# Attention and low-rank mixer in one kernel: the opening reordered, low-rank rows taken out of PSUM by ScalarE, V converted a step sooner, and narrower score tiles from step nine

## The chip, the cores and the metric

The kernel runs on one core of a Trainium2 chip. The metric is the device time of one execution in microseconds, as the median of several runs. TensorE does the matrix products, VectorE (DVE), ScalarE (ACT) and GpSimd (POOL) the element-wise work, and SyncE (SP) issues most of the DMAs; a few are issued by ScalarE.

## The reference, cut to what matters

A causal linear attention with a decay per head runs over blocks of 64 rows, and its output, with the heads side by side, goes through a low-rank mixing over the sequence and a two-layer product with a relu:

```
q, k, v: 4 batches x 8 heads x 768 rows x 64;  lam: one decay per head, 0.97 to 0.99
for each block of 64 rows:
    intra = ((q k^T) * D) v          D[i, j] = lam^(i - j) where i >= j, else 0
    inter = (q * lam^(i + 1)) state
    state = lam^64 * state + (k * lam^(63 - i))^T v
x = the heads side by side: 4 x 768 x 512
h = x^T U V                          U: 768 x 32, V: 32 x 768
u = x + h^T
out = u + relu(u w1) w2              w1: 512 x 2048, w2: 2048 x 512
```

U, V, w1 and w2 arrive as 64-bit floats, whose two 32-bit words the kernel loads and turns into 32-bit floats itself.

## The kernel before, in words

**Attention.** The kernel works on blocks of 128 rows, six for each of the four batches: 24 steps, s = 0 to 23. The order of the instructions is written out by hand: the list `pieces` (L546 to L567) names for each step what is issued, and each engine works through its own queue in that order. In a step the pieces are:

- `prep(s + 1)`: TensorE transposes the next block of q and k into one PSUM bank each (tags pq and pk, L348), ScalarE copies them out (L351). For step 0 this is done in two halves, ahead of the list, by `turn_half` (L663 and L668).
- `scale(s + 1)`: GpSimd multiplies q's transpose by powers of lam, `qs` (L376), and the k of the step after by others, `ks` (L365). The powers come from VectorE: `constants` makes the decay mask by eight scans (L302), `rev` is its last column (L671), and `powers` makes `powq` by four more scans (L314).
- `mix`, `low`, `low_rows`, `next_of_low`: the low-rank part, see below.
- `intra(s)`: TensorE multiplies the masked scores by v (L446), ScalarE copies the sum out (L451).
- `state(s)`: TensorE makes the state's increment into `pkv` (L411), which shares the bank pk; VectorE adds the faded old state (L419, or copies in L417).
- `scores(s + 1)` (L393), `inter(s + 1)` (L434, reading `qs` and the state), `masked(s + 1)` (VectorE, L402) and `fade(s + 1)` (ScalarE, L385).
- `aside(s)`: pieces of the conversion of U, V and two tiles of w1, by a table of steps (L624 to L628). What they give to ScalarE is put off to `late`, in the next step. A conversion of 64-bit words is L154, L155 (VectorE), L160, L161 (ScalarE), L171, L179, L184 (VectorE); V's split follows in L598 (VectorE), two casts in L605 on ScalarE and two on VectorE, and subtractions in L609 on VectorE and GpSimd.
- `turn(s - 7)`: transposes a finished block of u (L516) and splits it (L521, L532, L535, L536).

**Low-rank part.** After each batch, in steps 6, 12 and 18 and a fourth time among the first units of the next stage, `low` sums x^T U into the bank pq (or a bank b2, the fourth time), as four groups of 32 rows and 128 columns (L461). `low_rows` takes the high bits out of PSUM into the temporary `p_h`, four VectorE instructions of 32 x 128 (L474). `next_of_low` then issues, at three places, two ScalarE copies (L485, L486), four VectorE subtractions that read PSUM again (L480), and one ScalarE copy (L489). `mix` (L499) reads all of these as one operand `p_hl`.

**Temporaries.** `tmp` hands out three buffers in turn (L99) to `p_h`, to `ut` in `turn` and, in the later blocks, to `uf` too. In those later blocks (from block 16) GpSimd's L529 reads `ut` and `uf`.

**Products.** With the attention nearly done, `hidden` runs u w1 in three passes of 32-bit products split into parts (L718, L728; ScalarE and VectorE take the sums out in L724 and L733), with the rest of the low-rank part between its products (L773 to L784). Then the second product (L851, L853, L855) ends the kernel.

**Opening.** The core asks for q by SyncE and for k by ScalarE, then for lam by ScalarE (L652 to L654). Matmuls on a block of zeros keep TensorE occupied (`keep_busy`, L661, L666). lam is spread over all partitions by a product with ones (L665) and copied by VectorE (L669).

Of the kernel before, what the change touches and what calls it, by code (L numbers as in the profile page):

```python
# [10 lines left out]
U32 = mybir.dt.uint32  # L11
AF = mybir.ActivationFunctionType
ALU = mybir.AluOpType
# [5 lines left out]
def kernel(  # L19
# [68 lines left out]
    def set_ends(t):  # L88
        nc.vector.memset(t[:, 0:1], 1151.0)
        nc.vector.memset(t[:, 1:2], 255.0 * (1 << 23))  # L90
        ends.append(t)
# [6 lines left out]
    def tmp(name):  # L98
        return wconv.tile([P, C], FP32, tag="tmp", bufs=3, name=name)  # L99
# [145 lines left out]
    def two_banks(name, tag):  # L245
        return psf.tile([P, 2, N], FP32, tag=tag, name=name)
# [14 lines left out]
    def parts(s):  # L261
        return 2 if s == 0 else 1
# [44 lines left out]
    def powers():  # L307
        nc.vector.memset(zeros, 0.0)
        for x in range(2):
            nc.vector.tensor_copy(  # L310
                out=lamh[x * D : (x + 1) * D, :], in_=lamb[x * D : (x + 1) * D, x::2]
            )
        for a in range(HP):
            nc.vector.tensor_tensor_scan(  # L314
                powq[:, a, :], lamh[:, a : a + 1].broadcast_to([P, P]),
                zeros.broadcast_to([P, P]), 1.0, ALU.mult, ALU.add,
            )
# [13 lines left out]

    def keep_busy(n):

        out = two_banks("idle", "px")[:, 0, 0:P]
        for i in range(n):
            nc.tensor.matmul(out=out, lhsT=blank, rhs=blank, start=True, stop=True)

    qts, kts = {}, {}

# [11 lines left out]
        nc.scalar.copy(ts[s][:, a0 : a0 + n, :], pt)  # L351

    def prep(s):
        for a0 in range(0, HP, HP // parts(s)) if s > 0 else ():
            for name in "qk":
                turn_half(s, a0, name)
        st[s].update(qt=qts.pop(s), kt=kts.pop(s))
        for name in "qk":
            load_next(name)
# [27 lines left out]
    def scores(s):  # L387
        qt, kt = st[s]["qt"], st[s]["kt"]
        st[s]["pss"] = pss = two_banks("pss", "pss").rearrange("p x (a i) -> p x a i", a=HP)
        for a in range(HP):  # L390
            for x in range(2):
                for rows in half if s >= 2 * NT else [slice(0, P)]:
                    nc.tensor.matmul(  # L393
                        out=pss[rows, x, a, :], lhsT=kt[half[x], a, rows],
                        rhs=qt[half[x], a, :], start=True, stop=True,
                    )
# [70 lines left out]

    def low_rows(b):

        pp, t = pps.pop(b), tmp("p_h")[0:R]  # L470
        h, h2, l, l2 = (p_hl[g * R : (g + 1) * R] for g in range(G))
        own = [(slice(g * R, (g + 1) * R), slice(g * P, (g + 1) * P)) for g in range(G)]
        for rows, cols in own:
            nc.vector.tensor_scalar(  # L474
                t[:, cols].bitcast(U32), pp[rows].bitcast(U32), HI, None, ALU.bitwise_and
            )

        def low_part():
            for rows, cols in own:
                nc.vector.tensor_tensor(  # L480
                    out=l[:, cols], in0=pp[rows], in1=t[:, cols], op=ALU.subtract
                )

        def spread():
            nc.scalar.copy(h, t)  # L485
            nc.scalar.copy(h2, t)  # L486

        def spread_low():
            nc.scalar.copy(l2, l.bitcast(FP32))  # L489

        pps[b] = [spread, low_part, spread_low]
# [52 lines left out]


    pieces = [("prep", 0), ("scale", 0), ("scores", 0), ("inter", 0), ("masked", 0)]  # L546
    pieces += [("powers", 0)]
    for s in range(NS):
        b, c = divmod(s, NT)
        done = s - NT - 1  # L550
# [19 lines left out]
    def load_next(name, engine=nc.sync):  # L570
        if waiting[name]:
            load(name, waiting[name].pop(0), engine)
# [3 lines left out]
        "prep": prep, "fade": fade, "scores": scores, "masked": masked, "inter": inter,  # L576
        "intra": intra, "state": state,
        "low": low, "low_rows": low_rows, "next_of_low": next_of_low, "mix": mix, "turn": turn,
        "scale": scale, "powers": lambda s: powers(), "turned": lambda s: turned.pop(s)(),
    }  # L580
    def v_steps():

        st = {}

        def dst():
            if "v" not in st:
                st["v"] = wconv.tile([P, C], FP32, tag="wf", name="vf")[0 : 2 * R, 0:SH]
            return st["v"]

        def parts(gs):  # L590
            for half in range(2):
                rows, cols = slice(half * R, (half + 1) * R), slice(half * SH, (half + 1) * SH)
                for g in gs:
                    yield v_hl[g * R : (g + 1) * R, cols], rows

        def five():
            st["t"] = t = wconv.tile([P, C], FP32, tag="wt", name="vt")[0 : 2 * R, 0:SH]
            nc.vector.tensor_scalar(  # L598
                t.bitcast(U32), st["v"].bitcast(U32), HI, None, ALU.bitwise_and
            )  # L600
            on_scalar(lambda: high(0))

        def high(g, copy=nc.scalar.copy):
            for out, rows in parts((g,)):
                copy(out, st["t"][rows])  # L605

        def low(g, engine):
            for out, rows in parts((g,)):
                engine.tensor_tensor(  # L609
                    out=out, in0=st["v"][rows], in1=st["t"][rows], op=ALU.subtract  # L610
                )

        halves = [moe_V[:, half * SH : (half + 1) * SH] for half in range(2)]
        return weight_steps(dst, halves, SH, 2 * R, in_parts=True) + [
            five, lambda: low(1, nc.vector), lambda: high(2, nc.vector.tensor_copy),
            lambda: low(3, nc.gpsimd),
        ]
# [5 lines left out]
    side = {}  # L623
    for steps, at in (  # L624
        (u_side, (-1, 1, 1, 2, 2)),
        (v_steps(), (0, 0, 3, 3, 4, 4, 4, 5, 4, 5)),
        (w1_steps(0, True), (3, 4, 5, 6, 8, 9, 10, 11, 12, 13, 14)),
        (w1_steps(1, True), (8, 9, 10, 11, 15, 16, 17, 18, 19, 20, 21)),  # L628
    ):
        assert len(steps) == len(at)  # L630
        for step, n in zip(steps, at):
            side.setdefault(n, []).append(step)
# [16 lines left out]
    nc.vector.memset(blank, 0.0)  # L649
    nc.vector.memset(lam_row[:, H:], 1.0)  # L650
    set_ends(vp[:, S + C : S + C + 2].bitcast(FP32))
    load_next("q", nc.sync)  # L652
    load_next("k", nc.scalar)
    nc.scalar.dma_start(out=lam_row[:, 0:H], in_=lam.unsqueeze(0))  # L654
    for name in "qkvkv":
        load_next(name)
    aside(-1)
    for name in "qkv":
        load_next(name)
    make_identity(nc, ident)  # L660
    keep_busy(4)  # L661
    for name in "qk":
        turn_half(0, 0, name)  # L663
    pl = two_banks("pl", "pss")[:, 0, 0:H]
    nc.tensor.matmul(out=pl, lhsT=lam_row[:, H:], rhs=lam_row[:, 0:H], start=True, stop=True)  # L665
    keep_busy(1)  # L666
    for name in "qk":
        turn_half(0, HP // 2, name)  # L668
    nc.vector.tensor_copy(out=lamb, in_=pl)  # L669
    constants()  # L670
    nc.vector.tensor_copy(out=rev, in_=mask[:, :, :, P - 1])  # L671
    scale_k(0)
    run.update(aside=aside, late=on_scalar_late)
# [280 lines left out]
```

## Time and profile before

| what | us |
|---|---|
| median of six runs | 676.73 |
| lowest and highest run | 676.59, 677.12 |
| the profiled execution | 677.31 |
| its span, first to last instruction | 675.5 |
| TensorE, matmuls, busy | 666.0 |
| VectorE busy | 499.0 |
| ScalarE busy | 277.3 |
| GpSimd busy | 113.8 |

All views are of one profiled execution, and times in them count from the start of its span. In a timeline row the columns are start, duration, engine and line, the operation, the written and the read tile, the shape and the count of instructions merged in the row; in brackets stands how long the engine was idle before and what ended the wait. PEld is the loading of weights, which runs beside matmuls. A matmul of 32-bit floats shows as two instructions. In the table by stretches the columns are the stretch, its length, then the busy time of TensorE, its weight loads, VectorE, ScalarE and GpSimd with instruction counts, TensorE's granted clock, the DMA share and GB/s.

### The profile page before, as it was taken

What the parts mean: (1) busy time and instruction counts of PE and PEld (TensorE: products, weight loads), DVE (VectorE), ACT (ScalarE), POOL (GpSimd) and SP (SyncE); (2) the same over time, 40 slices, a digit from 0 to 9 for tenths busy, and PEclk for the clock granted to TensorE, in tenths of its full rate; (3) what the DMA queues carried; (4) which work ended last, traced back from release to release, by engine and by line L of the source; (5) the groups of instructions that cost most, each with busy time, mean ns of one, the idle gap of its engine ahead of it and who ended that gap; (6) DMA issues with size and microseconds to landing.
All of it is one profiled execution on the core that took longest, in us unless ns stands there. A gap on an engine that the chain in (4) does not pass through costs nothing.

```text
span 675.5 us, 13172 instructions
## 1 busy us (share of the span) xinstructions
PE 666.0 (99%) x5124; PEld 545.1 (81%) x5124; DVE 499.0 (74%) x879; ACT 277.3 (41%) x513; POOL 113.8 (17%) x92
## 2 busy tenths in 40 slices
PE   8999999999999999999999999999999999999997
PEld 7888898787888888888888888888888888888886
DVE  4689999777999777777798255786586776865864
ACT  4665767544555444444455132232232322322320
POOL 3446767331000000000000000030030200300300
PEclk9999999999999999999999999999999999999999
DMA  9998994164777655565577999854353363453431
GB/s 213 209 232 222 230 224 128 49 221 142 252 264 243 234 202 203 202 203 203 202 251 258 317 320 376 308 176 159 94 203 108 110 201 95 150 162 95 158 91 62
DMA packets 131775, 131.27 MB, mean 194 GB/s; under 512 B 81346, under 2 KB 89794, under 8 KB 131714
## 3 DMA queue, kind: packets, MB, share of 16 engines
q1 hardware_dynamic: 130656, 130.18, 60.9%
q8 instruction: 40, 0.66, 0.4%
q10 hardware_dynamic: 1058, 0.26, 0.2%
q14 instruction: 21, 0.17, 0.1%
HBM read 80.09 MB, written 50.33 MB: 193 GB/s over the span
## 4 chain that ended last, share of the span: by engine, by line
PE 94%; DVE 3%; ACT 1%; issue 0%; DMA 0%; DVEq 0%; ACTq 0%
PE pz L718 27%; PE pz L853 13%; PE pz L851 13%; PE pd L728 13%; PE pd L855 13%; PE px L446 3%; PE pss L393 3%; PE put L516 2%; PE pq L348 1%; PE px L434 1%; PE pkv L411 1%; PE pk L348 1%; DVE sm L402 1%; PE pp L461 1%; PE pu L499 1%
## 5 line engine op out<-in xcount | busy, mean ns | idle before, releaser
L718 PE MATMUL pz<-u_hl,w 128*128 128x512 f32 x768 | 190.3, 397 | 0.7 <-ACT x_nat L451 0.7
L718 PEld LDWEIGHTS pz<-u_hl,w 128*128 128x128 f32 x768 | 144.0, 188 | 36.0 <-ACT x_nat L451 0.8
L853 PE MATMUL pz<-w_hl,m 128*128 128x512 f32 x384 | 151.1, 396 | 0.0
L851 PE MATMUL pz<-w_hl,m 128*128 128x512 f32 x384 | 150.9, 396 | 0.0
L855 PE MATMUL pd<-w_d,m 128*128 128x512 f32 x384 | 149.5, 396 | 0.0
L834 ACT ACTIVATE m<-mt 128x512 fp32r<-128x512 f32 x96 | 60.6, 632 | 196.3 <-PE pd L855 145.9
L835 DVE SCALAR_TENSOR_TENSOR m<-rm,m 128x512 fp32r<-128x512 f32 x96 | 71.4, 746 | 51.7 <-ACT m L834 51.6
L880 POOL TENSOR_TENSOR o<-o,u 128x512 f32<-128x512 f32 x20 | 29.8, 1523 | 447.4 <-DVE o L876 447.4
L733 DVE SCALAR_TENSOR_TENSOR r<-pd,r 128x512 f32<-128x512 f32 x96 | 61.8, 686 | 53.7 <-ACT r L724 38.8
L728 PE MATMUL pd<-u_d,w 128*128 128x512 f32 x384 | 98.6, 397 | 0.0
L724 ACT ACTIVATE r<-pz 128x512 f32<-128x512 f32 x96 | 52.2, 596 | 93.4 <-PE pz L718 92.7
L853 PEld LDWEIGHTS pz<-w_hl,m 128*128 128x128 f32 x384 | 72.3, 188 | 17.7
L851 PEld LDWEIGHTS pz<-w_hl,m 128*128 128x128 f32 x384 | 72.3, 188 | 17.6
L855 PEld LDWEIGHTS pd<-w_d,m 128*128 128x128 f32 x384 | 72.3, 188 | 17.6
L728 PEld LDWEIGHTS pd<-u_d,w 128*128 128x128 f32 x384 | 72.1, 188 | 17.3
L836 DVE SCALAR_TENSOR_TENSOR m<-m 128x512 fp32r<-128x512 f32 x96 | 69.0, 720 | 0.9
L833 DVE TENSOR_SCALAR mt<-rm 128x512 uint32<-128x512 uint32 x96 | 46.1, 481 | 28.6 <-DMA rm<-r_d 27.7
L402 DVE TENSOR_TENSOR sm<-pss,mask 128x512 f32<-128x512 f32 x48 | 30.8, 683 | 5.1 <-PE pss L393 4.9
L205 ACT CAST w<-wt 128x512 fp32r<-128x512 f32 x32 | 19.9, 621 | 30.5 <-DVE wt L202 23.4
L446 PEld LDWEIGHTS px<-vraw,sm 128*64 128x64 f32 x768 | 24.7, 137 | 6.8 <-DVE sm L402 3.5
L376 POOL TENSOR_TENSOR qs<-qt,powq 128x512 f32<-128x512 f32 x20 | 26.0, 1298 | 23.9 <-ACT qt L351 22.0
L446 PE MATMUL px<-vraw,sm 128*64 128x64 f32 x768 | 28.6, 226 | 1.0 <-DVE sm L402 0.5
(85 smaller groups left out, 684.6 us busy)
## 6 DMA issues: line engine op xcount, KB each, us to landing
r_d<-r SPq DMA_DIRECT2D x96, 256.0 KB, 2.6
rm<-r_d SPq DMA_DIRECT2D x96, 256.0 KB, 2.7
words<-in_moe_w_ch_dram SPq DMA_DIRECT2D x30, 512.0 KB, 4.0
w_d<-w SPq DMA_DIRECT2D x16, 768.0 KB, 3.3
w_hl<-w_d SPq DMA_DIRECT2D x16, 512.0 KB, 6.4
vraw<-in_v_dram SPq DMA_DIRECT2D x24, 256.0 KB, 4.1
u_d<-x_nat SPq DMA_DIRECT2D x24, 256.0 KB, 3.6
u<-u_d SPq DMA_DIRECT2D x24, 256.0 KB, 4.1
```

What stands on the lines that cost most here:

```text
L446: nc.tensor.matmul(out=px[half[t], x, a, :], lhsT=sm[:, x, a, half[t]], rhs=vr[:, 2 * a + x, :], start=(first and a == 0), stop=(a == HP - 1),
L718: nc.tensor.matmul(out=acc[g][0], lhsT=w[:, n, ct, :], rhs=uhl[g][:, n, ct, :], start=(ct == 0 and n == 0), stop=(ct == CT - 1 and n == 1),)
L724: nc.scalar.mul(rs[g], acc[g][0], 4096.0 + 1.0)
L728: nc.tensor.matmul(out=acc[g][1], lhsT=w[:, 2, ct, :], rhs=ud[g][:, ct, :], start=(ct == 0), stop=(ct == CT - 1),)
L733: nc.vector.scalar_tensor_tensor(rs[g], acc[g][1], 4096.0, rs[g], ALU.mult, ALU.add)
L833: nc.vector.tensor_scalar(t.bitcast(U32), r.bitcast(U32), HI, None, ALU.bitwise_and)
L834: nc.scalar.activation(out=m[:, 0], in_=t, func=AF.Relu)
L835: nc.vector.scalar_tensor_tensor(m[:, 1], r, 0.0, hi, ALU.max, ALU.subtract)
L836: nc.vector.scalar_tensor_tensor(m[:, 2], hi, E, low, ALU.mult, ALU.subtract)
L851: nc.tensor.matmul(out=pz, lhsT=m[:, 0, cols], rhs=hl[:, 0], start=first, stop=False)
L853: nc.tensor.matmul(out=pz, lhsT=m[:, 1, cols], rhs=hl[:, 1], start=False, stop=end)
L855: nc.tensor.matmul(out=pd, lhsT=m[:, 2, cols], rhs=dd, start=first, stop=end)
```

## The change

Four things change. In the opening, lam is asked for ahead of q and k, on ScalarE's queue; q's and k's first transposes all come after lam's product and after two and then four matmuls on zeros (which now go to the bank pq, lam's product to a bank of tag pt); `powers` is issued ahead of `rev` and no longer after the first masking. In `low_rows` ScalarE copies the four groups out of PSUM into a new temporary `p_f`, and VectorE takes the high bits of all of it in one instruction of 32 x 512 and later subtracts in another. V's conversion and split are issued one step sooner, from L154 on; its loads stay. And the scores are made on halves of 64 rows from step 9, no longer from step 12.

```diff
     def keep_busy(n):
 
-        out = two_banks("idle", "px")[:, 0, 0:P]
+        out = one_bank([P, C], "idle", "pq")
         for i in range(n):
-            nc.tensor.matmul(out=out, lhsT=blank, rhs=blank, start=True, stop=True)
+            nc.tensor.matmul(out=out[:, 0:P], lhsT=blank, rhs=blank, start=True, stop=True)
...
     def prep(s):
-        for a0 in range(0, HP, HP // parts(s)) if s > 0 else ():
+        for a0 in range(0, HP, HP // parts(s)):
...
     def scores(s):
-                for rows in half if s >= 2 * NT else [slice(0, P)]:
+                for rows in half if s >= NT + 3 else [slice(0, P)]:
...
     def low_rows(b):
-        pp, t = pps.pop(b), tmp("p_h")[0:R]
+        pp, t, rows_f = pps.pop(b), tmp("p_h")[0:R], tmp("p_f")[0:R]
...
         for rows, cols in own:
-            nc.vector.tensor_scalar(
-                t[:, cols].bitcast(U32), pp[rows].bitcast(U32), HI, None, ALU.bitwise_and
-            )
+            nc.scalar.copy(rows_f[:, cols], pp[rows])
+        nc.vector.tensor_scalar(t.bitcast(U32), rows_f.bitcast(U32), HI, None, ALU.bitwise_and)
 
         def low_part():
-            for rows, cols in own:
-                nc.vector.tensor_tensor(
-                    out=l[:, cols], in0=pp[rows], in1=t[:, cols], op=ALU.subtract
-                )
+            nc.vector.tensor_tensor(out=l, in0=rows_f, in1=t, op=ALU.subtract)
...
-    pieces += [("powers", 0)]
...
-        (v_steps(), (0, 0, 3, 3, 4, 4, 4, 5, 4, 5)),
+        (v_steps(), (0, 0, 2, 2, 3, 3, 3, 4, 3, 4)),
...
+    nc.scalar.dma_start(out=lam_row[:, 0:H], in_=lam.unsqueeze(0))
     load_next("q", nc.sync)
     load_next("k", nc.scalar)
-    nc.scalar.dma_start(out=lam_row[:, 0:H], in_=lam.unsqueeze(0))
...
     make_identity(nc, ident)
+    keep_busy(2)
+    pl = one_bank([P, H], "pl", "pt")
+    nc.tensor.matmul(out=pl, lhsT=lam_row[:, H:], rhs=lam_row[:, 0:H], start=True, stop=True)
     keep_busy(4)
-    for name in "qk":
-        turn_half(0, 0, name)
-    pl = two_banks("pl", "pss")[:, 0, 0:H]
-    nc.tensor.matmul(out=pl, lhsT=lam_row[:, H:], rhs=lam_row[:, 0:H], start=True, stop=True)
-    keep_busy(1)
-    for name in "qk":
-        turn_half(0, HP // 2, name)
     nc.vector.tensor_copy(out=lamb, in_=pl)
     constants()
+    powers()
     nc.vector.tensor_copy(out=rev, in_=mask[:, :, :, P - 1])
```

More of the change, by code (lines that the diff above doesn't have):

```diff
@@ L578 @@
         "low": low, "low_rows": low_rows, "next_of_low": next_of_low, "mix": mix, "turn": turn,
-        "scale": scale, "powers": lambda s: powers(), "turned": lambda s: turned.pop(s)(),
+        "scale": scale, "turned": lambda s: turned.pop(s)(),
     }
```

## The prediction, made before the changed kernel had run

> **What bounds the kernel now.** I read the shares of busy time, the chain that ended last, TensorE's busy time by stretches, then the order of time through the attention steps.
>
> ```profile
> PE 666.0 (99%) x5124; PEld 545.1 (81%) x5124; DVE 499.0 (74%) x879; ACT 277.3 (41%) x513; POOL 113.8 (17%) x92
> ...
> PE 94%; DVE 3%; ACT 1%; issue 0%; DMA 0%; DVEq 0%; ACTq 0%
> ```
> ```profile
> 124.70:175.00 50.30, 50.29 (x272) 40.31 (x273) 38.76 (x72) 25.35 (x44) 11.61 (x9) 1.00 0.48 161
> 175.00:225.00 50.00, 50.00 (x215) 40.17 (x215) 47.69 (x88) 28.53 (x49) 0.00 (x0) 1.00 0.71 252
> ```
>
> The chain is 94% TensorE, and from 124.7 us its column is full. Every edit but one acts before that, and a microsecond gained or lost there passes unchanged to the end. So I price holes in TensorE's sequence in the first 133 us, and nothing else. A busy column hides short holes, so I measure from one step's start of the same matmuls to the next one's.
>
> **Part 1: the opening (lam first, TensorE kept busy, powers early).**
>
> ```profile
> 1.86 0.61 ACTq L654 DMA_DIRECT2D lam_row<-in_lam_dram  x1
> ...
> 6.69 2.00 PE L393 MATMUL pss<-qt,kt 64*128 64x128 f32 x16
> ...
> 8.74 1.29 DVE L402 TENSOR_TENSOR sm<-pss,mask 128x512 f32<-128x512 f32 x2 [0.41 <-PE pss L393]
> ...
> 10.73 1.37 DVE L314 TENSOR_TENSOR_SCAN powq<-small 128x128 f32<-128x128 f32 x4
> ...
> 12.25 1.26 POOL L376 TENSOR_TENSOR qs<-qt,powq 128x512 f32<-128x512 f32 x1 [1.75 <-DVE powq L314]
> ```
>
> The reader is to see that powq ends at 12.10, GpSimd's qs waits for it and ends at 13.51, and TensorE's L434 starts at 13.57. The scores before it started at 11.52; in later steps L434 follows them by 1.09 (60.84 to 61.93), so it could have started at 12.61: a hole of 0.96.
>
> Moved ahead, powers costs VectorE 0.06 (memset) + 2 x 0.17 (copies) + 1.37 (scans) = 1.8. It must fit between the mask and sm. lam's DMA moves from 1.86 to 0.73; its landing is not shown. Bounds: data move from about 1.9 (first busy slices of the DMA view), and lam's matmul L665 started at 4.59, at most 2.73 after issue, so 3.46 at the latest. I take 2.85, since q's 128 KB, issued at 0.74, let L348 start at 3.58. L665 then takes 0.52 (4.59 to 5.11), four fills 8 x 0.22 = 1.75, four half transposes 4 x 0.44 = 1.75, and the idle before the scores 0.33: scores start at 7.2, not 6.69. k's halves are asked for 0.6 later (lam's issue, 0.61); they were used at 4.03 and are now used after 5.5, so this is covered.
>
> The scores' passes are slow there: two every 0.213 until about 8.45, while warm steps have 0.136; the granted clock reads 1.00 throughout, so the row, not the clock column, shows it. Six pairs slow, two fast: sm starts near 9.05, 0.3 later. VectorE: lamb at 3.5, mask 2.64, powers 1.8, rev 0.2 ends near 8.4: before sm, covered. ks on GpSimd then runs 8.7 to 10.8 and qs to 12.1, in time for L434 at 12.9. **Sum: +0.3 - 0.96 = -0.65.** Ends: -1.3 (lam at 2.4, transition early) and +0.3 (lam at 3.46, transition unchanged, one extra VectorE delay).
>
> [...]
>
> **Part 2: V a step sooner.** Step 3 gains L154, L155, L171 on VectorE (0.34 + 0.35 + 0.55 = 1.24) after L184 ends at 24.2, ending at 25.45; state's L419 is due at 26.17: covered. ScalarE gains L160 and L161 after L451 at 26.12, 1.24 together, so faded runs 27.36 to 28.4 and qt's copy at 28.45 is just met: nothing.
>
> Step 4 gains L179 0.54, L184 0.55, L598 0.35 and the two L605 casts (1.43, measured beside GpSimd): 28.40 + 2.95 = 31.35, and behind them waits L419, which ran at 30.46. TensorE's L434, at 31.36, needs it (0.42): it starts at about 31.85. **+0.45**, between 0.1 (casts without GpSimd at half) and 0.6. ScalarE's two L605 casts (1.03) move to a step without faded: nothing. Step 5 gets VectorE's L609 (1.90) after sm, with no state that step, and GpSimd's L609 (2.18) between ks and ks: nothing. What goes with them, L609 at 37.02 ahead of the low-rank rows, belongs to part 3.
>
> **Part 3: low-rank rows, first time (step 6).**
>
> ```profile
> 38.95 1.23 DVE L474 TENSOR_SCALAR p_h<-pp 32x128 uint32<-32x128 uint32 x4
> ...
> 40.67 1.25 DVE L480 TENSOR_TENSOR vp<-pp,p_h 32x128 fp32r<-32x128 f32 x4
> ...
> 41.97 0.66 PE L348 MATMUL pq<-ident,qraw 128*128 128x128 f32 x4 [0.49 <-DVE vp L480]
> ...
> 44.03 0.58 ACT L351 COPY kt<-pk 128x512 f32<-128x512 f32 x1
> ...
> 44.66 0.69 PE L411 MATMUL pkv<-vraw,ks 128*64 128x64 f32 x16 [0.28 <-ACT kt L351]
> ```
>
> L348 waits because q's transposes share the bank that L480 still reads; pkv waits because it shares k's bank, whose copy is late behind ScalarE's L489 and faded. From scores (39.58) to scores (45.27) are 5.69. The same pieces without waits, from the next step without put: 1.09 + 0.62 + 1.31 + 0.98 + 0.57 = 4.57. Holes: 1.12.
>
> After: ScalarE copies pp from 36.58 + 1.66 = 38.24 (1.66 is pp's start to L474 where that waits for nothing else, 68.18 to 69.84). A copy of 128 columns is not in the trace. From 128x256 at 0.372 and 128x512 at 0.587, one column costs 0.84 ns, so 0.265; L385's small operations follow each other at 0.24. Bounds for four: 0.75 and 1.49 (0.372 each). I take 1.06, nearest to the fit: done at 39.3. VectorE: mask 0.43 (L202's shorter duration), kv 0.42, subtract 0.68 (L210): done at 40.9 instead of 41.92. ScalarE then runs without a break: L451 39.3, and by the spacings of step 12 (0.48, 0.63, 0.65, 1.07, 0.47, 0.54) pkv at about 43.8, where TensorE is ready at 43.58. The bank is free at 39.3. Remaining hole 0.2 to 0.3. **-0.85**, between -1.1 and -0.4.
>
> **The second and third time (steps 12, 18).** ScalarE runs back to back from L451 (70.83) to kt, and pkv at 75.93 waits for it; VectorE's relief meets a queue that cannot move. The copies have 69.84 to 70.83, 0.99, for 1.06. **+0.05 each**, between 0 and +0.5.
>
> [...]
>
> **The fourth time, among the first big products.**
>
> ```profile
> 128.73 1.28 POOL L529 TENSOR_TENSOR u_hl<-uf,ut 128x512 fp32r<-128x512 f32 x1 [2.18 <-ACT uf L528]
> 129.12 1.47 PEld L718 LDWEIGHTS pz<-u_hl,w 128*128 128x128 f32 x7 [0.20 <-issue]
> ...
> 129.34 1.23 DVE L474 TENSOR_SCALAR p_h<-pp 32x128 uint32<-32x128 uint32 x4 [0.83 <-PE pp L461]
> ```
>
> The new tile p_f takes a third buffer of tag tmp. There are three: ut, uf, p_h, and the fourth, p_f, falls on ut, which GpSimd's L529 reads until 130.01. So the copies start at 130.07, not 129.34, with L485, L486, L489 and L724 queued behind. Copies 1.06, mask 0.5 with its handover, three casts 1.9: p_hl complete near 133.55; L499 needs it and had it at 132.60. Nothing else can fill TensorE. **+0.9**, between +0.2 (no wait on L529) and +1.3.
>
> **Part 4: scores on 64x64 tiles in steps nine to eleven.**
>
> ```profile
> 60.84 1.16 PE L393 MATMUL pss<-qt,kt 64*128 64x128 f32 x16
> ...
> 62.55 0.66 PE L516 MATMUL put<-ident,x_nat 128*128 128x128 f32 x4
> ...
> 111.00 1.10 PE L393 MATMUL pss<-qt,kt 64*64 64x128 f32 x32
> ...
> 112.50 0.65 PE L516 MATMUL put<-ident,x_nat 128*128 128x128 f32 x4
> ```
>
> From scores to put: 1.71 with halves of 128 columns, 1.50 with 64x64, twice the instructions included: 0.21 a step. Steps ten and eleven have no wait in them, so 0.42. In step nine sm starts at 53.12 behind VectorE's L154 and L155, which slow beside GpSimd (1.03 and 1.50, against 0.42 elsewhere), and intra follows sm: the gain is given back. **-0.42**, between 0 and -0.63.
>
> **Sum.** -0.65 + 0.45 - 0.85 + 0.1 + 0.9 - 0.42 = -0.47. The profiled execution took 677.31 around a span of 675.5 and would take 676.84; it lies 0.58 above the median of the runs, 676.73, so I forecast 676.3. 0.2% is 1.35 us, about what a measurement of this kernel can tell from no change.
>
> **Rivals.**
> (a) *Slower: the slow rate lasts longer in the opening.* Place: the passes between 8.5 and 12.6. Price: they come at about half rate, so the transposes (0.88), intra (1.08), pkv (0.47) and scores (1.09), 3.5 in all, take up to 3.5 more; sm and the copies hide about 1. Net +2.5 - 0.47 = +2, 678.8. It decides from a transition after about 10.2. [...] Chance 0.10.
> (b) *ScalarE is the bound.* Copies at 0.372: step 6 gains only 0.4, steps 12 and 18 lose 0.5 each, the fourth 1.3: -0.65 + 0.45 - 0.4 + 1.0 + 1.3 - 0.42 = +1.3, 678.0. For: ScalarE has no break from L451 to kt. Against: 0.265 by the fit. Chance 0.10, in the middle class by a hair.
> (c) *The holes only move* (the change does not do what it says): step 6's waits turn into ScalarE's (gain 0.4), L434's hole is eaten by a later sm: +0.5 to +0.2, 677.0. Chance 0.20.
> (d) *Everything goes well:* opening -1.3, fourth time +0.2, V +0.2: -1.3 + 0.2 - 0.85 + 0.1 + 0.2 - 0.42 = -2.1, 674.7; from -1.4 on it counts as this case. Chance 0.15.
> The forecast has 0.45. Faster by over 0.2%: 0.15; slower: 0.10; within: 0.75. The range, 675.0 to 678.1, takes in (b) and (c) and the upper half of (d); it leaves out (a) and the rest of (d), 0.17.
>
> **What would show it.** Right: scores begin near 7.2, L434 of step 1 about 0.65 earlier; L434 of step 5 late behind L419; no L480 wait at L348, ScalarE unbroken in step 6; a hole of 0.9 before L499 near 133; 1.50 from scores to put in steps nine to eleven. Wrong: fast passes much before or after 8.4, copies far from 0.265, or p_f's copies starting right after pp.

## The result and the profile after

| | before | after |
|---|---|---|
| median of the runs, us | 676.77 (37 runs, 676.48 to 677.75) | **678.51** (17 runs, 676.82 to 681.25) |
| the profiled execution, us | 677.31 | 677.14 |
| its span, us | 675.5 | 675.3 |

The ratio is 1.0024, with a 95% interval of 1.0017 to 1.0031: the change makes the kernel 1.74 us slower, outside the range of the forecast (675.0 to 678.1). The profiled execution of the changed kernel is no slower than that of before, so it doesn't show the whole loss. The runs do: eleven of the 17 have a mean granted clock of 0.999 or 1.000, and their median is 677.60. The other six have 0.995 or 0.997, and the fastest of them took 678.86. What a mean of 0.997 stands for is seen below, in the profile of V alone: 3.41 us at half clock.

The edits shift line numbers. In views of after, L475, L478, L481, L482 and L485 are the mask, the subtraction and the three casts of the low-rank rows (before: L474, L480, L485, L486, L489), L495 is L499, L524 and L525 are L528 and L529, L593, L600 and L604 are L598, L605 and L609, and L710 is L718.

The page of after, its busy shares and its chain by engine:

```profile
PE 664.5 (98%) x5174; PEld 544.3 (81%) x5174; DVE 497.9 (74%) x855; ACT 281.3 (42%) x529; POOL 113.4 (17%) x92
...
PE 95%; DVE 3%; ACT 1%; issue 1%; DVEq 0%; ACTq 0%
```

TensorE is still the chain, but the share of "issue" in it, time with nothing to wait for, has risen from 0% to 1%. The view of TensorE's waits over the first 134 us says where it stood still (the columns after the names are us in total, times, longest us):

```profile
PE px L434 <- DVE kv L419: 2.0, 1, 2.0
PE px L434 <- issue: 1.8, 2, 1.0
```

Neither line is in the same view of before with more than 0.3 us. To place them I compare the moment at which each step's scores start (L393) in the two profiled executions. The last row is the first big product, L718 before and L710 after.

| scores of step | before | after | after is ahead by |
|---|---|---|---|
| 0 | 6.69 | 6.46 | 0.23 |
| 1 | 11.52 | 10.55 | 0.97 |
| 2 | 16.76 | 14.84 | 1.92 |
| 4 | 25.98 | 23.41 | 2.57 |
| 5 | 30.27 | 28.27 | 2.00 |
| 6 | 34.10 | 34.12 | -0.02 |
| 7 | 39.58 | 39.59 | -0.01 |
| 8 | 45.27 | 44.71 | 0.56 |
| 12 | 65.32 | 64.37 | 0.95 |
| 13 | 71.18 | 70.22 | 0.96 |
| 14 | 76.54 | 76.23 | 0.31 |
| 18 | 95.02 | 94.70 | 0.32 |
| 20 | 106.24 | 106.32 | -0.08 |
| first big product | 124.71 | 124.00 | 0.71 |

**The opening** gains about 1.9 us here. The timeline of after:

```profile
2.21 0.59 PE L658 MATMUL pl<-lam_row 1*128 1x8 f32 x2
...
6.04 1.37 DVE L314 TENSOR_TENSOR_SCAN powq<-small 128x128 f32<-128x128 f32 x4
...
6.46 1.27 PE L393 MATMUL pss<-qt,kt 64*128 64x128 f32 x16
...
9.59 1.26 POOL L376 TENSOR_TENSOR qs<-qt,powq 128x512 f32<-128x512 f32 x1
```

It is 1.92 ahead at step 2's scores; the further 0.65 to step 4 is a pause of TensorE in before (ahead of 23.15) that after does not have, see the pauses for instructions below. lam's product runs at 2.21, the powers are done at 7.41, ahead of sm, and qs ends at 10.85: L434 of step 1 no longer waits for it. The scores took 1.27 and not 2.00, since TensorE's rate had doubled at 5.99 and not at 8.49 (the start of the first record of the clock in each trace). In after the matmuls of L348's half transposes follow each other by 0.21 us from 5.36 to 6.00, and by 0.11 from there on.

**V a step sooner** then loses all of it: 0.57 between the scores of steps 4 and 5, and 2.02 between those of 5 and 6, where the moved pieces of steps 3 and 4 lie. The timeline of after around the second:

```profile
27.11 1.27 POOL L376 TENSOR_TENSOR qs<-qt,powq 128x512 f32<-128x512 f32 x1 [3.58 <-ACT qt L351]
27.21 1.39 DVE L593 TENSOR_SCALAR vt<-vf 64x384 uint32<-64x384 uint32 x1
...
28.63 2.16 DVE L600 CAST vp<-vt 32x384 fp32r<-32x384 f32 x2
29.59 2.06 POOL L604 TENSOR_TENSOR vp<-vf,vt 32x384 fp32r<-32x384 f32 x2
30.82 0.42 DVE L419 TENSOR_TENSOR kv<-pkv,faded 128x256 f32<-128x256 f32 x1
...
31.39 0.69 PE L434 MATMUL px<-kv,qs 64*64 64x64 f32 x32 [1.96 <-DVE kv L419]
```

L593, the split's first operation, took 1.39 us while GpSimd made qs; before, at a time when GpSimd was at rest, the same operation took a quarter of that. The rows of before that the prediction priced, and L419 with L434 behind it:

```profile
28.40 0.34 DVE L154 TENSOR_SCALAR sc<-words 64x384 uint32<-64x384 uint32 x1
...
30.46 0.42 DVE L419 TENSOR_TENSOR kv<-pkv,faded 128x256 f32<-128x256 f32 x1 [0.86 <-PE pkv L411]
...
31.37 0.69 PE L434 MATMUL px<-kv,qs 64*64 64x64 f32 x32
...
33.85 0.35 DVE L598 TENSOR_SCALAR vt<-vf 64x384 uint32<-64x384 uint32 x1
...
34.24 1.43 DVE L605 CAST vp<-vt 32x384 fp32r<-32x384 f32 x2
```

The two casts took 2.16 beside GpSimd, where the prediction had 1.43. L419 stands behind both, and TensorE's L434 behind L419. In step 3 it is the same on a smaller scale: L154 ran 1.42 us beside qs, 0.34 in before.

The ends of these operations say more than their lengths. L593 ended at 28.60, 0.22 after GpSimd's qs; L154 ended 0.21 after the qs of its step; the two casts, 1.10 and 1.05 us, ended 0.22 and 0.21 after the GpSimd operations that they met. In the row of 1.43 the first cast took 0.35, ahead of GpSimd's first subtraction, and the second 1.07, till 0.22 after that subtraction's end. So in all five cases an operation of 0.34 to 0.35 us was done 0.2 us after the GpSimd operation that it met, and took between 1.05 and 1.42 us by where in it it began.

**The low-rank rows.** First time and fourth time in after:

```profile
38.18 1.06 ACT L474 COPY p_f<-pp 32x128 f32<-32x128 f32 x4 [1.15 <-PE pp L461]
...
40.17 1.19 DVE L478 TENSOR_TENSOR vp<-p_f,p_h 32x512 fp32r<-32x512 f32 x1
```
```profile
128.21 1.28 POOL L525 TENSOR_TENSOR u_hl<-uf,ut 128x512 fp32r<-128x512 f32 x1 [1.60 <-ACT uf L524]
...
128.79 1.06 ACT L474 COPY p_f<-pp 32x128 f32<-32x128 f32 x4 [0.72 <-PE pp L461]
...
132.36 0.19 PEld L495 LDWEIGHTS pu<-vp 128*128 128x128 f32 x1 [0.43 <-ACT vp L485]
```

The four copies took 1.06 us, the very sum that was estimated. Step 6 gains 0.57. The fourth time, the copies start at 128.79, while GpSimd's L525 runs to 129.49: they do not wait for it. The last cast, L485, still comes late, and TensorE's L495 waits 0.43 for it. From the start of pp to L495 are 5.21 us, to L499 in before 4.92: 0.29 is lost. In the kernel with this part alone, steps 12 and 18 lose 0.09 and 0.05 up to the scores two steps on.

**The scores.** The scores of steps 10 and 11 gain 0.2 each, those of step nine nothing. But later steps lose, for instance step 13, by a pause in the middle of a run of like matmuls:

```profile
71.15 0.41 PE L434 MATMUL px<-kv,qs 64*64 64x64 f32 x16
...
72.60 0.46 PE L434 MATMUL px<-kv,qs 64*64 64x64 f32 x16 [1.04 <-issue]
```

L434's 32 instructions break off halfway, with nothing to wait for that the profile shows. The trace has packets of kind instruction (16 KB each, in queue q8), and one of them took 2.46 us, from 68.80 to 71.26; the matmuls go on 1.34 us after its end. A second pause, 0.76 us, ends at 102.81, 1.35 after the end of another (101.46).

**Not foreseen at all:** the first big product no longer waits. Before it stood 0.69 us behind ScalarE's L451, whose bank it takes; after it has no wait.

### The profile page after: what moved, and what is told of

It is laid out like the page before. It is cut to its first block, busy times and chain, and to the rows that moved or that the text cites. A ratio compares the mean times of both kernels' runs of the same rounds, so it can differ in the third digit from the quotient of the medians.

```text
span 675.3 us, 13262 instructions
## 1 busy us (share of the span) xinstructions
PE 664.5 (98%) x5174; PEld 544.3 (81%) x5174; DVE 497.9 (74%) x855; ACT 281.3 (42%) x529; POOL 113.4 (17%) x92
## 4 chain that ended last, share of the span: by engine, by line
PE 95%; DVE 3%; ACT 1%; issue 1%; DVEq 0%; ACTq 0%
PE pz L710 27%; PE pz L845 13%; PE pz L843 13%; PE pd L720 13%; PE pd L847 13%; PE px L446 3%; PE pss L393 3%; PE put L512 2%; PE pq L348 1%; PE px L434 1%; PE pkv L411 1%; PE pk L348 1%; PE pp L461 1%; DVE sm L402 1%; PE pu L495 1%
## 5 line engine op out<-in xcount | busy, mean ns | idle before, releaser
L710 PE MATMUL pz<-u_hl,w 128*128 128x512 f32 x768 | 190.5, 397 | 0.0
L710 PEld LDWEIGHTS pz<-u_hl,w 128*128 128x128 f32 x768 | 144.0, 188 | 35.5 <-issue 0.4
L446 PEld LDWEIGHTS px<-vraw,sm 128*64 128x64 f32 x768 | 24.6, 137 | 6.3 <-DVE sm L402 2.4
L446 PE MATMUL px<-vraw,sm 128*64 128x64 f32 x768 | 28.2, 226 | 0.7 <-DVE sm L402 0.6
```

The source lines that it names most:

```text
L446: nc.tensor.matmul(out=px[half[t], x, a, :], lhsT=sm[:, x, a, half[t]], rhs=vr[:, 2 * a + x, :], start=(first and a == 0), stop=(a == HP - 1),
L710: nc.tensor.matmul(out=acc[g][0], lhsT=w[:, n, ct, :], rhs=uhl[g][:, n, ct, :], start=(ct == 0 and n == 0), stop=(ct == CT - 1 and n == 1),)
```

## The experiments

The first theory was that V's step alone is the loss: the hole in front of L434, and the half clock that it brings in some runs. The rivals: the runs spread because the opening's slow rate ends at a different moment each time (theory 2), or the loss is in ScalarE's copies and the pauses (theory 3). The first four kernels do one part alone, or undo one. Each is told with its median, lowest and highest time, and its ratio to the runs of before on the same chip. Differences in us are to the median of those runs, which lies between 676.75 and 677.03.

### V a step sooner, alone

```diff
-        (v_steps(), (0, 0, 3, 3, 4, 4, 4, 5, 4, 5)),
+        (v_steps(), (0, 0, 2, 2, 3, 3, 3, 4, 3, 4)),
```

> The kernel before with V's conversion a step sooner, nothing else. Theory 1 (V's pieces on VectorE beside GpSimd hold back the state of step 4, and the 2 us hole this leaves on TensorE sometimes brings a stretch of lowered granted clock): slower by 2 to 4 us, about 678.8 to 680.5, runs spread over 3 us or more, some with a mean granted clock of 0.997 or less. Theory 2 (the spread comes from the opening, whose slow rate ends at a different moment each time): slower by 0.5 to 2.5 us, spread no wider than before's 1.3 us, every clock at 0.999 or 1.000. Theory 3 (ScalarE's copies and TensorE's stalls for nothing shown): no change, 676.8, tight.

Measured: 679.18 (678.98 to 680.71, 5 runs), ratio 1.0041 (1.0028 to 1.0053), so +2.36 us. Three runs at a clock of 1.000 lie at 678.98 to 679.18; two at 0.997 took 680.51 and 680.71. The profiled execution is one of the latter. Its table by stretches, and two executions of the same group L446 in its timeline:

```profile
30.00:35.00 5.00, 3.04 (x74) 2.74 (x70) 4.89 (x7) 1.68 (x4) 4.73 (x5) 1.00 0.88 204
35.00:40.00 5.00, 4.97 (x59) 4.21 (x57) 1.90 (x4) 1.97 (x4) 0.00 (x0) 0.66 1.01 235
```
```profile
28.88 1.15 PE L446 MATMUL px<-vraw,sm 128*64 128x64 f32 x32
...
33.55 0.69 PE L434 MATMUL px<-kv,qs 64*64 64x64 f32 x32 [1.96 <-DVE kv L419]
...
35.31 1.98 PE L446 MATMUL px<-vraw,sm 128*64 128x64 f32 x32
```

TensorE is idle 1.96 us ahead of 33.55; from 35.03 on, for 3.41 us, it has half the clock (granted clock 0.66 in the stretch), and the same 32 matmuls take 1.98 us and not 1.15. The three runs at full clock lost 2.2 to 2.4 us, which is about what V's two waits take (0.50 ahead of the L434 before this one, and 1.96 here); in two of five the half clock takes some 1.5 us more.

Why two of five and not all? In the traces the records of TensorE's clock, but for the last, which ends with the trace, last whole multiples of 3.413 us: 665.6 us is 195 of them, 78.51 is 23 and 23.89 is 7, and at half clock 3.41 is one and 6.83 two. Continued from the first record, this grid has boundaries at 31.61 and 35.02 here, so nearly the whole hole (31.59 to 33.55) lies in one period, and half clock starts with the next. In the profile of after the hole is as long (29.43 to 31.39), but a boundary at 29.88 parts it into 0.45 and 1.51, and no half clock follows. So of two holes of 1.96 us the one that lies nearly whole in one period of this grid was followed by half clock, and the one that a boundary parts was not. That rests on these two profiles and the one with a larger hole below; what sets the clock isn't shown.

### The opening alone

```diff
+        out = one_bank([P, C], "idle", "pq")
...
+    nc.scalar.dma_start(out=lam_row[:, 0:H], in_=lam.unsqueeze(0))
     load_next("q", nc.sync)
     load_next("k", nc.scalar)
...
     constants()
+    powers()
```

Only three hunks are shown; all of the opening's stand in the section on the change.

> The kernel before with the new opening alone (lam first, fills and lam's product in other banks, powers early, step 0's transposes together). Theory 1: faster by 1.9 (the start of step 2) plus 0.7 (the first big product no longer waits for the last copy out of PSUM), about 674.2, spread of 1.5 us or less. Theory 2: spread of 3 us or more, median between 676 and 679. Theory 3: as theory 1.

Measured: 675.95 (674.69 to 677.01, 11 runs), ratio 0.9984 (0.9975 to 0.9993), so -0.87, a third of what was expected, with a spread of 2.3 us. All clocks 0.999 or 1.000. In its profiled execution the rate doubled at 6.06 and the scores of steps 1 and 2 started at 10.58 and 14.87, as in after.

### The low-rank rows alone

```diff
+            nc.scalar.copy(rows_f[:, cols], pp[rows])
+        nc.vector.tensor_scalar(t.bitcast(U32), rows_f.bitcast(U32), HI, None, ALU.bitwise_and)
...
+            nc.vector.tensor_tensor(out=l, in0=rows_f, in1=t, op=ALU.subtract)
```

> The kernel before with ScalarE copying the low-rank rows, nothing else. Theory 1 and 2: within 0.6 us of before (gain of up to 0.6 in step 6, loss of 0.4 the fourth time), tight. Theory 3: slower by 1 us or more, since ScalarE's queue grows and TensorE stalls by 1 us in steps 12 and 18.

Measured: 676.82 (676.56 to 677.81, 11 runs), the median of before to the digit; ratio 1.0001 (0.9992 to 1.0009). In the profile step 6 gains 0.57 and the fourth time loses 0.29.

### After, with V in its old steps

```diff
-        (v_steps(), (0, 0, 2, 2, 3, 3, 3, 4, 3, 4)),
+        (v_steps(), (0, 0, 3, 3, 4, 4, 4, 5, 4, 5)),
```

> The changed kernel with V's conversion back in its old steps. Theory 1: the two holes of steps 3 and 4 go (0.57 and 2.02) and with them the spread: 674 to 675, spread of 1.5 us or less, clocks at 0.999 or 1.000. Theory 2: the spread of the changed kernel stays, 3 us or more, median about 676. Theory 3: only the holes go, spread stays as the 1 us stalls do, median about 675.5.

Measured: 677.29 (676.63 to 678.42, 11 runs), ratio 1.0009 (1.0000 to 1.0018). By the first theory this should have been well below before, at 674 to 675; it is 0.5 above. The theory falls as the whole story: V's step is 1.2 of the loss, and something else eats the gain of the opening. One of the eleven runs has a clock of 0.997, though V's hole is gone. In the profile there are two pauses in L434, of 0.77 and 0.71 us, ending at 72.03 and 107.78, 1.28 and 1.43 after the end of an instruction packet. It also has something that the profiles of after and of before don't have. Twice ScalarE's L451 stands for 2.4 us because the block of x that it is to write over is still being stored (u_d<-x_nat), and its next copies come late; the second time TensorE waits for one of them:

```profile
65.29 0.58 ACT L451 COPY x_nat<-px 128x512 f32<-128x512 f32 x1 [2.43 <-DMA u_d<-x_nat]
...
66.94 1.52 PE L461 MATMUL pp<-x_nat,u_w 128*32 128x128 f32 x48 [0.77 <-ACT qt L351]
```

From scores to scores, steps 10 and 12, where L451 stands, took 0.80 and 0.70 more than in after; steps 13 and 20, with the pauses, 0.37 and 1.01 more than in before. So in this profile the store costs about as much as the pauses.

### Narrow scores from step nine, alone

```diff
-                for rows in half if s >= 2 * NT else [slice(0, P)]:
+                for rows in half if s >= NT + 3 else [slice(0, P)]:
```

> The kernel before with the scores on 64x64 tiles from step nine, nothing else. Theory 4 (TensorE's instructions are themselves fetched by DMA, 16 KB at a time; twice as many instructions in steps 9 to 11 make the fetch late, and TensorE stops about 1 us, ending 1.35 us after the fetch's last byte): in the profile one or two stalls of 0.7 to 1.3 at L434 for nothing shown, time 677 to 678, spread of 2 us. Rival (the arithmetic of the prediction, 0.21 in each of two steps): 676.4, tight, no such stall.

Measured: 677.37 (676.73 to 678.45, 11 runs), ratio 1.0007 (0.9998 to 1.0016): +0.34, where the forecast had -0.42. Its profile has one long pause in L434, ending at 92.20, 1.46 after a packet's end, and a short one at 72.05.

### The bank of the filling matmuls, alone

```diff
-        out = two_banks("idle", "px")[:, 0, 0:P]
+        out = one_bank([P, C], "idle", "pq")
```

> The kernel before with the fills written to the bank pq instead of px, which changes only the order in which the PSUM banks are first handed out. Theory 5 (the first big products then get a bank that has long been free, in place of px's, which ScalarE's L451 reads last): faster by 0.7, 676.1, and no wait of L718 for L451. Rival (the 0.7 came from elsewhere in the opening): 676.8, wait still there.

Measured: 676.32 (676.04 to 676.78, 11 runs), ratio 0.9989 (0.9980 to 0.9997): -0.71. In before, then in this kernel, the first big product:

```profile
124.71 1.20 PE L718 MATMUL pz<-u_hl,w 128*128 128x512 f32 x4 [0.69 <-ACT x_nat L451]
```
```profile
123.45 1.20 PE L718 MATMUL pz<-u_hl,w 128*128 128x512 f32 x4
```

In the built programs the fills, which come first, lie on bank 0. In before they are of tag px, and px lies on banks 0 and 1; here they are of tag pq, and px, first used much later, lies on banks 6 and 7. The first big product gets bank 0 in both, and its wait for L451's copy of px, 0.69 in before, is gone. That is worth 0.7 us, 115 us after the edited line. The new opening has the same effect in it, and 0.71 is most of the 0.87 that the opening alone gained.

### Opening and low-rank rows together

The hunks of those two experiments, one after the other; V and the scores as before.

> The kernel before with the new opening and ScalarE's copies, V and the scores as before. Theory 4 (the stalls come with the narrow scores): the opening's 675.95 less the 0.6 that the copies gain in step 6 plus 0.3 the fourth time, about 675.6, no stall of over 0.7 for nothing shown, spread no wider than the opening's 2.3. Rival (a faster front runs into the DMAs whatever its instructions): 676.5 to 677.5 as without V, with stalls or waits for u_d in the front.

Measured: 675.05 (674.66 to 675.58, 6 runs), ratio 0.9971 (0.9960 to 0.9983), -1.98. No pause for instructions in its profile. It differs from the kernel with V back by the scores alone: narrow scores from step nine cost 2.4 us on top of it, although they cost 0.34 on top of before. L451 waits for the store of x here too, four times and up to 1.5 us, but TensorE loses little by it (0.3 us in each of steps 13 and 15). In the profiles with the old opening ScalarE has no such wait, in four of the seven with the new one it has. Whether it is the narrow scores that make the waits costly, as in the kernel with V back, isn't shown.

### A hole of chosen size, in a place of no other change

```diff
+            for i in range(4 if s == 15 else 0):
+                nc.vector.tensor_tensor(out=spin, in0=mask[:, 0], in1=mask[:, 1], op=ALU.mult)
```

They stand ahead of L419 in before, and go to a tile that nothing reads. With the line that makes the tile, line numbers shift by three: L437 is L434, and L422 is L419.

> The kernel before with four extra VectorE products of 128x512 into a scratch tile in step 15, ahead of the state's addition; the output is that of the reference. It opens a hole of about 2.3 us on TensorE away from V and the opening. Theory 1 (a hole of 2 us on TensorE is enough for a stretch of half clock): slower by 2.3 us in most executions and by about 4 in some, whose mean granted clock is 0.997. Rival (the lowered clock needs what V does in step 4, or the opening): 679.1 in all, every clock at 0.999 or 1.000.

Measured: 680.57 (680.42 to 682.99, 5 runs), ratio 1.0062 (1.0049 to 1.0075). Two of five runs have clocks of 0.994 and 0.997 and took 682.99 and 681.80; the others took 680.42 to 680.57. The four products took 3.80 us beside GpSimd, so the hole was larger than planned. Its waits, and the stretch behind it in the profiled execution:

```profile
PE px L437 <- DVE kv L422: 3.3, 1, 3.3
```
```profile
90.00:95.00 5.00, 5.00 (x59) 4.44 (x61) 3.75 (x7) 2.09 (x6) 1.24 (x2) 0.50 0.15 35
```

For the whole of 90 to 95 us the clock is 0.50, with 59 matmuls. The half clock here ran for 6.83 us, from 88.86, while TensorE still stood, to 95.68. On the grid 2.20 us of the hole lie in the period before 88.86.

### Half of that hole

The same edit with `range(2 if s == 15 else 0)`.

> As the kernel with four extra VectorE products in step 15, but with two; the output is that of the reference. The hole on TensorE should be 1.2 to 1.9 us. Theory 1 with a threshold between this hole and the 2 us of V: slower by 1.2 to 2, every clock at 0.999 or 1.000, spread like before's. Rival (any hole of over 1 us brings half clock in some executions): one run or more in five at 0.997.

Measured: 678.48 (678.26 to 678.68, 11 runs), ratio 1.0023 (1.0014 to 1.0032); all clocks 0.999 or 1.000, all runs within 0.42 us. That is +1.57; in the profile step 16 took 1.24 longer than in before, though the row gives a wait of 0.9.

```profile
PE px L437 <- DVE kv L422: 0.9, 1, 0.9
```

So with a hole of 0.9 us no run of eleven had a clock below 0.999; with one of 2.0 us two of five (V alone) and six of 17 (after) had, with one of 3.3 us two of five.

### V's first pieces sooner, L598 and the casts at their old place

In before, V's table as below: L598 and the casts stay at their old place, the rest is issued a step sooner, so that only L179 and L184 stand ahead of L419 in step 4.

```diff
-        (v_steps(), (0, 0, 3, 3, 4, 4, 4, 5, 4, 5)),
+        (v_steps(), (0, 0, 2, 2, 3, 3, 4, 4, 4, 4)),
```

> The kernel before with V's first pieces a step sooner as in the change, but the split into parts (L598, both sets of casts, both subtractions) all in step 5's place behind sm, where no state waits; so only L179 and L184 (1.1 us) stand ahead of the state of step 4. Theory 1 (what costs is the 2.5 to 4 us of VectorE work queued ahead of L419, not V's being sooner): within 0.7 us of before, 676.4 to 677.6, no clock under 0.999. Rival (any earlier V collides with GpSimd or the DMAs): 678.5 or more.

Measured: 677.27 (677.18 to 677.72, 11 runs), ratio 1.0006 (0.9997 to 1.0015), with no run below a clock of 0.999. L598 and the casts ahead of L419 are therefore what costs 2.0 of V's 2.36 us.

### Opening, and the low-rank rows on ScalarE the first time only

```diff
-        "low_rows": low_rows,
+        "low_rows": lambda b: low_rows(b) if b else low_rows_by_scalar(b),
```

Here `low_rows_by_scalar` is the changed kernel's `low_rows`, and `low_rows` that of before.

> The new opening, and ScalarE's copies for the first low-rank rows alone (the other three as before), V and scores as before. Theory 6 (the copies pay in step 6 only, cost 0.1 in steps 12 and 18 each where ScalarE has no break, and 0.45 the fourth time, where L485 ends late): 675.05 less 0.5, about 674.5. Rival (the copies pay wherever they relieve VectorE): slower than the version with all four, 675.2 or more.

Measured: 674.99 (674.11 to 677.09, 11 runs), ratio 0.9974 (0.9966 to 0.9983). That is not to be told from the copies at all four times (675.05), so the 0.3 us of the fourth time don't show in the medians; in the profile they are saved (4.91 us from pp to L499).

### Narrow scores from step six, and from step ten

The edit of the scores with `s >= NT`, and with `s >= NT + 4`, each alone in before.

> The kernel before with scores on 64x64 tiles from step six. By the arithmetic of 0.21 a step in the steps that TensorE bounds (seven, eight, ten, eleven): faster by 0.6 to 0.8, 676.1. Theory 4 (late fetches of TensorE's own instructions, whose place depends on how many instructions went before): 676.5 to 678, with a stall of 0.7 or more at L434 that ends 1.3 to 1.45 after a fetch's end, at another place than with step nine.

> The kernel before with scores on 64x64 tiles from step ten. Step nine's gain was given back to VectorE anyway, so by the arithmetic this equals the kernel with step nine. Theory 4 (late fetches, set by how many instructions went before): differs from 677.37 by 0.5 or more, 676.4 if no fetch is late, since the remaining gain is 0.42. Rival (what is lost in the kernel with step nine comes from the narrow scores themselves): 677.2 to 677.5.

Measured: from step six 676.59 (676.18 to 677.49, 11 runs), ratio 0.9995 (0.9986 to 1.0004); from step ten 676.75 (676.19 to 677.81, 11 runs), ratio 1.0002 (0.9993 to 1.0011). Neither profile has a pause in L434 with nothing to wait for. Fewer of the expected microseconds show in the medians than arithmetic gives, and that part stays open.

### The opening with powers at the old place

```diff
     constants()
-    powers()
...
+    pieces += [("powers", 0)]
```

> The kernel before with the new opening, but powers issued after the first masking again. Theory 7 (the wide spread of the new opening comes from the moment at which TensorE's rate doubles, between 6 and 11 us; the hole behind powers, 0.96 in the kernel before, used to swallow it): spread of 1.2 us or less, median 675.5 to 676.2, with L434 of step 1 waiting for qs. Rival (the spread comes from the waits for u_d's DMA further on): spread as wide as the opening's, 2.3.

Measured: 675.13 (674.80 to 676.92, 11 runs), ratio 0.9980 (0.9971 to 0.9989). The median is lower than that of the whole opening (675.95): moving the powers ahead, which was the opening's main gain in the prediction, gains nothing that can be seen. L434 of step 1 waits 0.5 us for qs here. Whether late powers also narrow the spread is not settled: ten of eleven runs lie at or below 675.83, one at 676.92.

### The parts that gained, together

Opening, first low-rank rows on ScalarE, scores narrow from step six; V and the later low-rank rows as before.

> The fastest version so far (new opening, ScalarE's copies for the first low-rank rows alone) with scores on 64x64 tiles from step six. Theory 4 with a lucky place of the fetches: 674.99 less 0.3 to 0.6, 674.5; with an unlucky one 675.5 or more, with a stall that ends 1.3 to 1.45 after a fetch.

Measured: **674.16** (673.59 to 674.74, 5 runs), ratio 0.9961 (0.9948 to 0.9973). It beats both kernels, and its profile has no pause for instructions in L434.

### The pauses for instructions, over the profiled executions

From the traces: the pauses of L434 with nothing to wait for, and the last instruction packet that ended before them.

```
kernel                       L434 goes on   packet's end   later by
before                       23.15          21.75          1.40
after                        72.60          71.26          1.34
after                        102.81         101.46         1.35
after, V in its old steps    72.03          70.75          1.28
after, V in its old steps    107.78         106.35         1.43
scores from nine, alone      72.05          70.82          1.22
scores from nine, alone      92.20          90.74          1.46
```

By the rows the pause of before is 0.33 us and that at 72.05 is 0.35, the others 0.71 to 1.04. These seven are all the pauses of over 0.25 us with nothing to wait for between 8 and 125 us in the 17 profiles, and six of them are in the three kernels with scores from nine. The profiles of the scores from six and from ten have none (where L434 pauses there, it is for an operand). The reading that fits is that TensorE had run out of instructions and went on when the next 16 KB had arrived. The change adds instructions (on 64x64 tiles L393 counts 32 a step and not 16, and the page of after 5174 matmuls and not 5124), so where the packets fall among the matmuls moves.

What makes a packet late isn't shown. Each profile has 20 to 22 of them in that time, and few bring a pause; in the kernel with scores from ten a packet took 2.25 us, in the last one above 2.66, with no pause behind either. That the instructions are the cause rests on seven pauses with nearly the same distance; a kernel with lighter DMA traffic at those moments wasn't tried. Each profile is one execution, so how often a run meets such a pause isn't known.

## Why the prediction was wrong

Alone, the four parts measured -0.87 (opening), +2.36 (V), 0.00 (low-rank rows) and +0.34 (scores), +1.83 in sum; the change measured +1.74. That the two agree is luck: opening and low-rank rows together made -1.98, and on top of these the scores cost 2.4 and V 1.2. The forecast had -0.65, +0.45, +0.15 (the four terms of part 3: -0.85, twice +0.05, +0.9) and -0.42, -0.47 in sum.

- **Part 2 failed, and it is the largest miss:** "28.40 + 2.95 = 31.35 ... **+0.45**, between 0.1 ... and 0.6". The place and the mechanism were right: L434 behind L419 behind V's pieces. The size was not: 2.36. Two terms were mis-sized. L598 was counted at 0.35, from a row where GpSimd was at rest, and the casts at 1.43, from a row where one of the two had started ahead of GpSimd. At their new place they meet qs, ks and GpSimd's L609, and measured 1.39 and 2.16; L154 in step 3 measured 1.42 and not 0.34, so that "covered" wasn't true there, and L434 waited 0.50. And the half clock was priced only for the opening, as rival (a); here it came in the matmuls behind step 4's hole, of 1.96 us, in two runs of five.
- **Part 4 failed in sign:** "**-0.42**, between 0 and -0.63". The 0.21 a step were there, and step nine gave its share back as foretold. Not in the sum were the pauses of TensorE with nothing to wait for, and what a faster front meets: +0.34 alone, and some 2.4 on top of opening and low-rank rows. The profile of that kernel divides the loss about evenly between pauses and late copies behind the store of x; how the median divides stays open.
- **Part 1 was right in sign and size, in part by luck.** A gain that it did not have is the bank of the first big product (-0.71 alone); taken from the -0.87 it would leave next to nothing, but the other kernels with the new opening, and the scores as before, gained 1.6 to 2.0, so the two can't simply be subtracted. In after lam's product ran at 2.21, not 2.85, and over the seven profiles with the new opening the first scores started at 6.46 to 7.10, not 7.2. "A hole of 0.96" behind the powers was there, but it also hides a late doubling of the rate. Over the profiled executions the doubling came between 5.99 and 11.60; with the old opening the scores of step 2 started at 16.76 to 16.98 whatever it was, with the new one at 14.84 to 16.15. So the new opening passes on what the hole had swallowed: it gained 1.9 with the doubling at 5.99, in after's profile, and 0.6, the forecast's -0.65, with the doubling at 8.76. What sets the moment of the doubling no run shows.
- **Part 3 was right in kind.** The copies took 1.06, as estimated; ScalarE was not the bound (rival (b) falls); step 6 gained 0.57, in the range given and not 0.85, since the subtraction took 1.19 beside GpSimd and not 0.68, and pkv still waits 0.33 for ScalarE's copy of k. Steps 12 and 18 lost 0.09 and 0.05, as forecast. The fourth time lost 0.29, a third of the 0.9: "the copies start at 130.07" was wrong, they started at 128.79 right after pp. The three buffers of `tmp` are not handed out strictly in turn: p_f got the free one and p_h that of uf, so the copies did not have to wait for GpSimd's L529. In the median the part is 0.00.
- **The rivals.** (a) comes nearest in number (678.8 against 678.51), by luck: it put the loss in the opening, and with the new one no profile has the doubling after 8.76, where (a) needed 10.2. V back in its old steps takes 1.2 off the loss, and half clock came in six of 17 runs only. (c) is not what happened: step 6 kept its 0.57, and what took the opening's gain away in the profile were V's new holes, which (c) does not have. (d) is reached in number by the parts that gained, with scores from step six in place of nine: 674.16 against 674.7.

## What to carry to other kernels

Work put ahead of a state update on a vector engine is to be priced at the durations it has beside the neighbour that will run then, not at those of its old place (L598: 0.35 there, 1.39 beside GpSimd's qs); and behind a hole of 1.96 us in TensorE half clock took another 1.5 us here, in two runs of five, so what such a hole does is seen in the clocks of many runs, not in one profile. An edit that changes the order of allocations or the number of instructions acted far from its place here: by which bank a later product gets (0.7 us here), and, as far as the traces tell, by where the instruction packets fall (0.3 to 1.0 us a pause). Therefore measure each part alone, and then the parts that gain together.

## What the runs showed of the hardware that I had not expected

- V's L154, L598 and casts on VectorE, 0.34 to 0.35 us each and with both tiles in SBUF, ended 0.21 to 0.22 after the GpSimd operation during which they began (and took 1.05 to 1.42); a subtraction of 32 x 512, 0.68 alone, ended 0.54 and 0.55 after it (and took 1.19 and 1.25). L417, which reads pkv in PSUM, took 0.42 in the middle of GpSimd's ks (40.21 in before) and ended 0.16 ahead of it.
- The moment at which TensorE's rate doubles differed by 5.6 us (5.99 to 11.60) among profiled executions, also between kernels with the same opening (8.49 to 11.60).
- Behind a hole half clock came in pieces of 3.41 us (once 6.83, twice that), on a grid of 3.413 us. It set in 1.5 us after the end of one hole (of 1.96 us) and 1.1 ahead of the end of the other (of 3.31 us).
- TensorE stood though it waited for nothing that the profile shows: pauses of 0.3 to 1.0 us that end 1.22 to 1.46 us after a 16 KB packet of instructions, behind packets that took 0.9 to 2.5 us.
